# Infini-attention with a routed token: SP in emitted order, reordered projection jobs, and reads apart from writes

## The chip, the cores and the metric

The kernel runs on one core of one Trainium2 chip, in one launch. The metric is the device time of the launch in microseconds. The kernel before was timed in three runs: 855.94 us median (854.62 to 859.12). The profile that is read here is of one more execution, which took 853.65 us; its span, from the first recorded instruction to the last, is 851.4 us.

## The reference

```python
x = A_x                                   # 2048 tokens x 640, float32
g = sigmoid((x * gate_w).sum(-1, keepdims=True))
q, k, v = (heads of x @ wq, x @ wk, x @ wv)   # 32 heads of 20 columns, 4 segments of 512 tokens
for s in range(4):                        # M, z start at zero
    p = softmax(qs @ ks.T * scale + causal_mask)
    a_dot = p @ vs
    a_mem = phi(qs) @ M / (phi(qs) @ z + 1e-6)
    o_s = sig(beta) * a_mem + (1 - sig(beta)) * a_dot
    M += phi(ks).T @ vs ;  z += phi(ks).sum()
a = concat(o_s) @ wo
r = x @ w_r ; t = argmax(r)               # one routed token
y = (silu(x[t] @ w_gate) * (x[t] @ w_up)) @ w_down * sigmoid(r[t])
out = g * a + (1 - g) * (x with y added to row t)
```

## The kernel before

Products are kept near float32 by splitting each operand into `hi` (rounded) and `lo` (the rest), and adding three matrix products: hi·hi, hi·lo, lo·hi. The core runs everything on one stream of TensorE (PE) work, written out by hand.

**Units and jobs.** The heads are taken in two halves of 16, and in each half the four segments follow one another: 8 units `u`. The projections of a unit are nine jobs of 15 matmuls each, in the order `JOBS`: five jobs T0 to T4 (128 rows of q and k columns by 512 tokens, `acc` at L338) and four jobs V0 to V3 (128 tokens by 320 columns of v, `acc` at L343). `TILES` says which heads a T job holds; group 0 of the unit is complete after T1, group 1 after T2, group 2 after T3, group 3 after T4 (`LAST`).

**From a T job to the attention.** When a T job is done, `evac_t` writes `hi` (ScalarE, ACT) and `lo` (VectorE, DVE), and `place` stores both to a scratch in DRAM (`stkq`, `stkk`: L214, L216). When a group's q or k is complete there, `place` reads it back, rearranged, as the operands `qs` and `ks` (L220). There are `NS` = 5 such buffers for each.

**Groups and slots.** A group `n` is four heads of one segment, 32 in all. The main loop goes through groups in six slots each. In a slot `b_step` makes scores of group n (`bt`, L414; ACT takes their exponentials `p`, GpSimd, POOL, masks them), `a_step` makes scores of a group ahead, from which DVE takes the row maxima (`a` L383, `junk` L386), and `fill` emits projection matmuls until their progress in groups (`chunks`) is `LEAD` = 3.4 groups ahead of the slot. The maxima of group n+1 are split (`m_split`, `mneg`) in slot 3, transposed on PE (`m_rows`, `mtp` L399) in slot 4, copied by ACT (`mr`) and written by four small DMAs into two rows of that group's `qs` (L404). The first `bt` of group n+1 needs them. `pv_step` multiplies the exponentials with v in slots 5 and 1; `norm` divides in slot 2 and stores the group to DRAM (`otok`, L462).

**The rest.** At group 15 `route` finds the routed token, with eight small DMAs that each need the one before (`rrow`, `row`, `sel`, `all`, twice); from group 16 on the three products of its SwiGLU run beside the attention, with weights loaded in pairs (`wt`, L521). From group 28 on `out_proj` multiplies the stored rows with `wo`: for each 128 tokens it loads `ot` and `xf` (`row_load`, `out_load`), transposes (`ttp`, L600), multiplies (L625) and stores (L634). At the start of each of its four segments the loads and the transposes are emitted one right behind the other.

**What sets the order.** All DMAs are issued by SyncE (SP), one after the other: an issue whose data or buffer isn't ready holds all that stand behind it. PE alone runs in the order in which the program emits its instructions (`manual_schedule`, L85). For SP, DVE, ACT and POOL a scheduler sorts the instructions, by its own estimate of when each can start. At the start `prepare_t` loads and splits the weights of all five T jobs (a group's columns once for each job that needs a part of them), and those of V, before the first matmul is emitted (L664 to L672).

Of the kernel before, what the change touches and what calls it, by code (L numbers as in the profile page):

```python
# [18 lines left out]
KT = D // 128  # L19
# [24 lines left out]
)  # L44
QGROUP = {0: 0, 1: 1, 3: 2, 4: 3}
JOBS = ("T0", "T1", "V0", "V1", "T2", "V2", "V3", "T3", "T4")
LAST = {"T1": 0, "T2": 1, "T3": 2, "T4": 3}


# [5 lines left out]
def tile_infini_mod(  # L55
# [26 lines left out]
    def f32(t):  # L82
        return t.bitcast(F32)

    ctx.enter_context(tc.manual_schedule(engines={mybir.EngineType.PE}))  # L85


    jp = one.tile([128, 128], I32, name="jp")
# [73 lines left out]

    def prepare_t(hf, j, eng=None):

        hi, lo = w_tile(("T", hf, j))
        for i, (r0, r1, kind, g, c0) in enumerate(TILES[j]):
            t = pool.tile([128, KT, 4, DH], F32, tag="raw", bufs=4, name="raw")
            nc.sync.dma_start(t.rearrange("p k j d -> p k (j d)"), columns(kind, hf, g, GC).rearrange("(k p) m -> p k m", p=128))
            src = t[:, :, :, c0 // 4:(c0 + r1 - r0) // 4].rearrange("p k j d -> p k d j")
            h_, l_ = (f32(w).rearrange("p (k m) -> p k m", k=KT)[:, :, r0:r1].rearrange("p k (d j) -> p k d j", j=4)  # L170
                      for w in (hi, lo))
            split(h_.bitcast(F32R), l_.bitcast(F32R), src, eng or nc.vector)

    def load_w(key):
        if key[0] == "V":
# [31 lines left out]

    def place(kind, m, c0, hi, lo, r0, n):

        assert m - NS < current[0]  # L210
        d = stk[kind][m % NS]
        first, gap, low = {"q": (0, GC, 2 * GC), "k": (0, 2 * GC, GC)}[kind]
        src = f32(hi)[r0:r0 + n, :L]
        nc.sync.dma_start(bass.AP(tensor=d.tensor, offset=d.offset + (first + c0) * L, ap=[[L, n], [gap * L, 2], [1, L]]),  # L214
                          bass.AP(tensor=src.tensor, offset=src.offset, ap=[list(src.ap[0]), [0, 2], list(src.ap[1])]))
        nc.sync.dma_start(d[low + c0:low + c0 + n, :], f32(lo)[r0:r0 + n, :L])  # L216
        if c0 + n == GC:
            dst = f32((qs if kind == "q" else ks)[m % NS])
            for b in range(2):
                nc.sync.dma_start(dst[64 * b:64 * b + ST].rearrange("r p t -> r (p t)"),  # L220
                                  d.rearrange("(r b p) t -> r b (p t)", b=2, p=2)[:, b])
# [77 lines left out]
    def prefetch(u, job):  # L299

        hf, s = divmod(u, SEG)
        if s == SEG - 1:
            at = {"T0": 0, "T1": 1, "T2": 2, "T3": 3, "T4": 4}.get(job)
            if at is not None and hf + 1 < NH:
                prepare_t(hf + 1, at)
            elif at is not None:
                load_w(("O", at))
                split_w(("O", at))
        if u + 1 < NU:
            for k in {"T3": (0, 1), "T4": (2, 3, 4)}.get(job, ()):  # L310
                load_x(u + 1, k)
                if k < 2:
                    split_x(u + 1, k)
        if u == SEG and job == "T0":
            for k in range(KT):
                load_w(("V", 1, k))
                split_w(("V", 1, k))

    def projections():
        total = 15 * (5 * L + 4 * VC)  # L320
        old = 0
        for u in range(NU):
            hf, s = divmod(u, SEG)
            done = 0
            for job in JOBS:
                j = int(job[1])
                prefetch(u, job)
                acc = psum.tile([128, L], F32, tag="misc", bufs=3, name="acc")
                w = L if job[0] == "T" else VC + (2 if hf == 0 else 0)
                more = rest(old)  # L330
                i = 0
                for k in range(KT):
                    xh, xl = X[u, k]
                    for part in range(3):
                        if job[0] == "T":
                            wh, wl = (t[:, 128 * k:128 * k + 128] for t in W["T", hf, j])
                            a, b = ((wh, xh), (wl, xh), (wh, xl))[part]
                            nc.tensor.matmul(acc, a, b, start=i == 0, stop=i == 3 * KT - 1)  # L338
                        else:
                            wh, wl = (t[:, :w] for t in W["V", hf, k])  # L340
                            h_, l_ = xh[:, 128 * j:128 * j + 128], xl[:, 128 * j:128 * j + 128]
                            a, b = ((h_, wh), (h_, wl), (l_, wh))[part]
                            nc.tensor.matmul(acc[:, :w], a, b, start=i == 0, stop=i == 3 * KT - 1)  # L343
                        i += 1
                        done += w
                        chunks[0] = 4 * (u + min(done / total, 1.0))
                        yield w * COST_MM
                        if i in (4, 7, 10, 13):
                            cost = next(more, 0.0)
                            if cost:  # L350
                                yield cost
                    if job == "T4" and u + 1 < NU and k < 3:
                        split_x(u + 1, k + 2)
                yield from more
                old = len(tail)
                if job[0] == "T":
                    evac_t(u, j, acc)
                else:
                    evac_v(u, j, acc)
                if job in LAST:  # L360
                    groups[0] = 4 * u + LAST[job] + 1
                if job == "T4" and s < SEG - 1:
                    tail.append(memory_write(u))
        yield from rest(len(tail))
        chunks[0] = 4.0 * NU + 100
# [81 lines left out]
    def norm(n):  # L447
# [10 lines left out]
        nc.vector.tensor_tensor(out=ou, in0=tp[:, :, :, :DH], in1=sub(rs, 0, [[4, 4], [1, 4], [0, DH]]), op=OP.mult)  # L458
        if s > 0:
            nc.gpsimd.tensor_tensor(out=ou, in0=ou, in1=om.pop(n), op=OP.add)  # L460
        c0 = DH * (HH * hf + 4 * g)
        nc.sync.dma_start(otok[L * s:L * s + L, c0:c0 + GC].rearrange("(c p) e -> p c e", p=128),  # L462
                          ou.rearrange("p c j d -> p c (j d)"))

# [200 lines left out]
    for k in range(KT):  # L665
        load_x(0, k)
        split_x(0, k, nc.vector if k % 2 else nc.gpsimd)
    for j in range(1, KT):
        prepare_t(0, j)
        if j == 1:  # L670
            for k in range(KT):
                load_w(("V", 0, k))  # L672
                split_w(("V", 0, k))
    proj = Fill(projections())

    extra = []
    side = []
    LEAD = 3.4

    def fill(at):  # L680
        proj.until(lambda: chunks[0] >= at / 6 + LEAD)
# [16 lines left out]
    for n in range(-2, NG):  # L698
        for slot in range(6):
# [13 lines left out]
            if n >= -1:  # L713
                fill(6 * n + slot)
            if slot == 3 and 0 <= n + 1 < NG:
                m_split(n + 1)
            if slot == 4 and 0 <= n + 1 < NG:
                m_rows(n + 1)
            if n >= -1:
                fill(6 * n + slot + 0.5)  # L720
            if n >= 1 and slot == 2:
                norm(n - 1)
                ready[0] = n - 1
            if n == 15 and slot == 0:
                route()
# [8 lines left out]

    pv_step(NG - 1, 1)
    extra[0].run(4000)
    norm(NG - 1)
    ready[0] = NG - 1
    extra[0].finish()
    Fill(out_proj(3)).finish()  # L740
# [40 lines left out]
```

## Time and profile before

| | |
|---|---|
| median of 3 runs | 855.94 us |
| profiled execution: its time, its span | 853.65 us, 851.4 us |
| PE busy | 701.1 us (82%) |
| DVE, ACT, POOL busy | 453.7 (53%), 360.5 (42%), 188.9 (22%) us |
| mean granted clock of PE | 0.895 of 2.4 GHz |
| DMA moved | 117.95 MB, 139 GB/s mean |
| chain that ended last | PE 51%, DMA 23%, DVE 9%, ACT 7%, SP 5% |

How to read it: PE is busy most of the span, so time is lost where it stands still, and where its clock is granted at half. "A <- B" means that A's engine stood idle until B was done. A bracket at the end of a timeline row is that idle time. SPq is SP's issue of DMAs; a row of several issues lasts as long as they took together, waits between them included. Where an issue waits, the row before ends and the next one starts late.

### The profile page before, as it was taken

The page shows a single profiled execution, that of the slowest core. Times are in us where ns is not written, and L with a number is a line of the kernel's source. Part 1 is how long each engine was busy: PE and PEld are TensorE (multiplying, and loading weights), DVE is VectorE, ACT ScalarE, POOL GpSimd, SP SyncE. Part 2 cuts the span into 40 slices and gives each one's busy share as a digit, 9 for nine tenths or more (in the row PEclk, how much of TensorE's full clock was granted, in tenths as well). Part 3 has the DMA queues.
Part 4 walks back from the last instruction along what each step waited for, and adds up shares of the span by engine and source line. Part 5 has one row for each costly group of instructions (what it writes and reads, how often), then busy time and mean ns, then how long its engine had stood idle before and what let it go on. Part 6 is the DMA issues. An engine that isn't in the chain of part 4 may idle for free.

```text
span 851.4 us, 13366 instructions
## 1 busy us (share of the span) xinstructions
PE 701.1 (82%) x4496; PEld 469.2 (55%) x4496; DVE 453.7 (53%) x1523; ACT 360.5 (42%) x608; POOL 188.9 (22%) x297
## 2 busy tenths in 40 slices
PE   5067789987998899668978889777988998899998
PEld 2045356644754565435644555445554665777787
DVE  6324546555555566345654546563564666474354
ACT  4312434454544455344443434433452545344422
POOL 4010412142213233322231111331241222111100
PEclk9569889988998999679988989889997999799999
DMA  6632633264426445566246635665445565443453
GB/s 181 178 117 61 185 113 94 70 175 137 103 70 171 112 114 148 144 173 137 70 125 175 195 118 157 197 194 155 118 113 155 156 161 164 115 142 104 146 178 125
DMA packets 85876, 117.95 MB, mean 139 GB/s; under 512 B 42726, under 2 KB 46320, under 8 KB 85808
## 3 DMA queue, kind: packets, MB, share of 16 engines
q1 hardware_dynamic: 85808, 117.10, 49.3%
q8 instruction: 36, 0.59, 0.3%
q14 instruction: 32, 0.26, 0.1%
HBM read 74.58 MB, written 41.96 MB: 137 GB/s over the span
## 4 chain that ended last, share of the span: by engine, by line
PE 51%; DMA 23%; DVE 9%; ACT 7%; SPq 5%; issue 4%; POOL 0%; ACTq 0%; DVEq 0%
PE acc L338 13%; PE acc L343 7%; PE pv L434 6%; PE acc L625 6%; PE bt L414 6%; DMA ks<-stkk 6%; PE a L383 5%; DVE junk L386 4%; DMA qs<-mr 4%; DMA stkq<-lo 3%; DMA stkk<-lo 3%; DMA xf<-in_x_dram 2%; SPq L220 2%; PE nm L253 2%; SPq L404 2%
## 5 line engine op out<-in xcount | busy, mean ns | idle before, releaser
L386 DVE CUSTOM_DVE_ANT_0 junk<-a,mask 128x512 bf16<-128x512 f32 (+3 forms) x512 | 250.6, 489 | 178.7 <-PE a L383 168.2
L418 ACT ACTIVATE p<-bt 128x768 f32<-128x768 f32 (+1 forms) x192 | 169.6, 883 | 211.4 <-PE bt L414 209.0
L421 POOL TENSOR_SCALAR_AFFINE_SELECT p<-p 128x256 f32<-128x256 f32 (+1 forms) x192 | 94.6, 493 | 421.3 <-ACT p L418 417.8
L383 PE MATMUL a<-ks,qs 60*128 60x256 f32 (+2 forms) x512 | 98.1, 375 | 73.8 <-DMA ks<-stkk 55.0
L414 PE MATMUL bt<-qs,ks 62*128 62x256 f32 (+2 forms) x512 | 105.9, 425 | 40.8 <-DMA qs<-mr 34.1
L414 PEld LDWEIGHTS bt<-qs,ks 62*128 62x128 f32 x512 | 50.1, 199 | 101.5 <-issue 61.2
L383 PEld LDWEIGHTS a<-ks,qs 60*128 60x128 f32 x512 | 54.3, 204 | 91.5 <-issue 38.4
L338 PE MATMUL acc<-xhi,whi 128*128 128x512 f32 x200 | 92.3, 461 | 9.2 <-ACT xhi L148 8.0
L338 PE MATMUL acc<-xhi,wlo 128*128 128x512 f32 x200 | 94.7, 474 | 0.2 <-DVE wlo L149 0.2
L338 PE MATMUL acc<-xlo,whi 128*128 128x512 f32 x200 | 92.4, 462 | 1.2 <-POOL xlo L149 1.0
L434 PE MATMUL pv<-p,va 128*32 128x512 f32 (+3 forms) x1024 | 87.9, 465 | 0.0
L149 POOL TENSOR_TENSOR xlo<-raw,xhi 128x512 fp32r<-128x512 f32 x38 | 48.2, 1275 | 76.6 <-ACT xhi L148 72.2
L338 PEld LDWEIGHTS acc<-xhi,whi 128*128 128x128 f32 x200 | 42.4, 212 | 30.6 <-issue 14.5
L343 PE MATMUL acc<-wlo,xhi 128*128 128x322 f32 (+1 forms) x160 | 56.5, 353 | 0.0
L338 PEld LDWEIGHTS acc<-xlo,whi 128*128 128x128 f32 x200 | 42.4, 212 | 23.7 <-issue 15.3
L625 PE MATMUL acc<-whi,oh 128*128 128x320 f32 x160 | 53.3, 333 | 2.3 <-ACT oh L602 1.1
L343 PE MATMUL acc<-whi,xhi 128*128 128x322 f32 (+1 forms) x160 | 54.6, 341 | 0.3 <-ACT mr L401 0.3
L343 PE MATMUL acc<-whi,xlo 128*128 128x322 f32 (+1 forms) x160 | 52.0, 325 | 0.0
L625 PE MATMUL acc<-whi,ol 128*128 128x320 f32 x160 | 51.7, 323 | 0.3 <-DVE ol L603 0.3
L338 PEld LDWEIGHTS acc<-xhi,wlo 128*128 128x128 f32 x200 | 43.3, 217 | 15.6 <-issue 9.3
L434 PEld LDWEIGHTS pv<-p,va 128*32 128x32 f32 x1024 | 28.3, 115 | 40.2 <-issue 30.1
L625 PE MATMUL acc<-wlo,oh 128*128 128x320 f32 x160 | 50.2, 313 | 0.0
(104 smaller groups left out, 923.8 us busy)
## 6 DMA issues: line engine op xcount, KB each, us to landing
qs<-stkq SPq DMA_DIRECT2D x64, 240.0 KB
ks<-stkk SPq DMA_DIRECT2D x64, 240.0 KB
raw<-in_xT_dram SPq DMA_DIRECT2D x40, 256.0 KB
stkq<-hi SPq DMA_DIRECT2D x32, 320.0 KB
stkq<-lo SPq DMA_DIRECT2D x32, 160.0 KB
otok<-ou SPq DMA_DIRECT2D x32, 160.0 KB
ot<-otok SPq DMA_DIRECT2D x16, 320.0 KB
xf<-in_x_dram SPq DMA_DIRECT2D x16, 320.0 KB
```

Source lines behind the costliest of these rows:

```text
L149: eng.tensor_tensor(out=lo, in0=raw, in1=f32(hi), op=OP.subtract)
L220: nc.sync.dma_start(dst[64 * b:64 * b + ST].rearrange("r p t -> r (p t)"), d.rearrange("(r b p) t -> r b (p t)", b=2, p=2)[:, b])
L253: nc.tensor.matmul(nm[:, c, :], e[:GC, 128 * c:128 * c + 128], mbd[:, g, :], start=True, stop=True)
L338: nc.tensor.matmul(acc, a, b, start=i == 0, stop=i == 3 * KT - 1)
L343: nc.tensor.matmul(acc[:, :w], a, b, start=i == 0, stop=i == 3 * KT - 1)
L383: nc.tensor.matmul(a[:, b, at:at + nw], q_, k_, start=True, stop=True)
L386: nc.vector.tensor_tensor_reduce(out=junk[:, :w], in0=a[:, b, at:at + w], in1=mask[:, L - w:], scale=1.0, scalar=-3e38, op0=OP.add, op1=OP ...
L414: nc.tensor.matmul(bt[:, b, at:at + nw], k_, q_, start=True, stop=True)
L418: nc.scalar.activation(pt, bt[:, :, at:at + w], AF.Exp, scale=SCALE)
L421: nc.gpsimd.affine_select(out=d, in_=d, pattern=[[0, 2], [0, k], [1, 128]], base=0, channel_multiplier=-1, compare_op=OP.is_ge, fill=0.0)
L434: nc.tensor.matmul(pv[n][32 * j:32 * j + 32, L - w:], va[u % 2][:, c, VW * h:VW * h + 32], pt_tiles[n, j % 2, min(c, 2)][:, j // 2, at:at ...
L625: nc.tensor.matmul(acc[:, :n], a_[:, 128 * k:128 * k + 128], b_[:, n * b:n * b + n], start=i == 0, stop=i == 3 * KT - 1)
```

## The change

SP, too, keeps the order in which the program emits. With that the program emits its DMAs elsewhere: weights are loaded by groups of heads (`READY`; one load feeds every T job that holds a part), and those of the first unit job by job ahead of their use; `place` only writes, and the reads of the operands are gathered (`backs`) and emitted by `bring_back` at the sixth matmul of the next job, from where on the group counts as landed. `JOBS` and the prefetches are reordered, `LEAD` is 3.7, `m_split` and `m_rows` stand one slot earlier, and the store of a group one slot after its `norm`.

```diff
+READY = (("q", 0), ("k", 0)), (("q", 1), ("k", 1)), (("k", 2),), (("q", 2), ("k", 3)), (("q", 3),)
-JOBS = ("T0", "T1", "V0", "V1", "T2", "V2", "V3", "T3", "T4")
+JOBS = ("T0", "T1", "T2", "V0", "V1", "T3", "V2", "T4", "V3")
...
-    ctx.enter_context(tc.manual_schedule(engines={mybir.EngineType.PE}))
+    ctx.enter_context(tc.manual_schedule(engines={mybir.EngineType.PE, mybir.EngineType.SP}))
...
     def prepare_t(hf, j, eng=None):
-        hi, lo = w_tile(("T", hf, j))
-        for i, (r0, r1, kind, g, c0) in enumerate(TILES[j]):
+        for kind, g in READY[j]:
             t = pool.tile([128, KT, 4, DH], F32, tag="raw", bufs=4, name="raw")
...
+            for i, tl in enumerate(TILES):
+                for r0, r1, kind_, g_, c0 in tl:
+                    if (kind_, g_) != (kind, g):
+                        continue
+                    hi, lo = W.get(("T", hf, i)) or w_tile(("T", hf, i))
...
     def place(kind, m, c0, hi, lo, r0, n):
...
         if c0 + n == GC:
+            backs.append((kind, m))
+
+    backs = []
+
+    def bring_back():
+        while backs:
+            kind, m = backs.pop(0)
+            assert m - NS < current[0]
+            d = stk[kind][m % NS]
             dst = f32((qs if kind == "q" else ks)[m % NS])
             for b in range(2):
                 nc.sync.dma_start(dst[64 * b:64 * b + ST].rearrange("r p t -> r (p t)"),
                                   d.rearrange("(r b p) t -> r b (p t)", b=2, p=2)[:, b])
...
     def prefetch(u, job):
-            at = {"T0": 0, "T1": 1, "T2": 2, "T3": 3, "T4": 4}.get(job)
+            at = {"T1": 0, "T2": 1, "V0": 2, "V2": 3, "V3": 4}.get(job)
...
-            for k in {"T3": (0, 1), "T4": (2, 3, 4)}.get(job, ()):
+            for k in {"T4": (0, 1), "V3": (2, 3, 4)}.get(job, ()):
...
-        if u == SEG and job == "T0":
-            for k in range(KT):
-                load_w(("V", 1, k))
-                split_w(("V", 1, k))
+        if u == 0:
+            j = {"T0": 1, "T1": 2, "V0": 3, "V1": 4}.get(job)
+            if j is not None:
+                prepare_t(0, j)
...
+                        if i == 6:
+                            bring_back()
+                            groups[0] = landed
+                            if (u, job) in ((0, "T2"), (SEG, "T0")):
+                                for kk_ in range(KT):
+                                    load_w(("V", hf, kk_))
+                                    split_w(("V", hf, kk_))
...
-                    groups[0] = 4 * u + LAST[job] + 1
+                    landed = 4 * u + LAST[job] + 1
...
-    for j in range(1, KT):
-        prepare_t(0, j)
-        if j == 1:
-            for k in range(KT):
-                load_w(("V", 0, k))
-                split_w(("V", 0, k))
...
-    LEAD = 3.4
+    LEAD = 3.7
...
             if slot == 3 and 0 <= n + 1 < NG:
-                m_split(n + 1)
-            if slot == 4 and 0 <= n + 1 < NG:
                 m_rows(n + 1)
             if n >= -1:
                 fill(6 * n + slot + 0.5)
+            if slot == 2 and 0 <= n + 1 < NG:
+                m_split(n + 1)
             if n >= 1 and slot == 2:
-                norm(n - 1)
+                done = norm(n - 1)
+            if n >= 1 and slot == 3:
+                store(n - 1, done)
                 ready[0] = n - 1
```

Three places on SP show what moves. The first is the start of the program: the rows up to the first store of an operand, of the kernel before and then of the changed one (`raw<-in_wc` is a load of weights, `stkq`, `stkk` the scratch, `qs`, `ks` the operands).

```order
L168 DMA raw_242<-in_wc_dram 128x5x80
L168 DMA raw_246<-in_wc_dram 128x5x80
L168 DMA raw_252<-in_wc_dram 128x5x80
L168 DMA raw_256<-in_wc_dram 128x5x80
L214 DMA stkq0_71<-hi_276 80x2x512
L216 DMA stkq0_71<-lo_277 80x512
L214 DMA stkk0_76<-hi_276 48x2x512
L216 DMA stkk0_76<-lo_277 48x512
L220 DMA qs0_106<-stkq0_71 60x1024 x2
```

```order
L168 DMA raw_176<-in_wc_dram 128x5x80
L168 DMA raw_180<-in_wc_dram 128x5x80
L218 DMA stkq0_71<-hi_204 80x2x512
L220 DMA stkq0_71<-lo_205 80x512
L218 DMA stkk0_76<-hi_204 48x2x512
L220 DMA stkk0_76<-lo_205 48x512
L168 DMA raw_216<-in_wc_dram 128x5x80
L233 DMA qs0_106<-stkq0_71 60x1024 x2
L218 DMA stkq1_72<-hi_242 80x2x512
```

Before, 25 issues of weights stand between the last load of `xT` and the first store; now two do. The second place is in unit 1, where a T job's operands are stored and read, with the four small writes of the maxima (`qs<-mr`) behind them; of the kernel before, then of the changed one.

```order
L214 DMA stkq2_73<-hi_1472 80x2x512
L216 DMA stkq2_73<-lo_1473 80x512
L214 DMA stkk2_78<-hi_1472 48x2x512
L216 DMA stkk2_78<-lo_1473 48x512
L220 DMA qs2_112<-stkq2_73 60x1024 x2
L220 DMA ks2_113<-stkk2_78 60x1024 x2
L404 DMA qs0_106<-mr_1493 1x8x128 x4
```

```order
L218 DMA stkq2_73<-hi_1373 80x2x512
L220 DMA stkq2_73<-lo_1374 80x512
L218 DMA stkk2_78<-hi_1373 48x2x512
L220 DMA stkk2_78<-lo_1374 48x512
L144 DMA raw_1385<-in_xT_dram 128x512
L144 DMA raw_1387<-in_xT_dram 128x512
L144 DMA raw_1389<-in_xT_dram 128x512
L233 DMA qs2_112<-stkq2_73 60x1024 x2
L233 DMA ks2_113<-stkk2_78 60x1024 x2
L424 DMA qs0_106<-mr_1500 1x8x128 x4
```

The reads stood right behind the writes that they need, and the maxima right behind the reads; now three loads stand between writes and reads. The third place is the last segment of `out_proj`: loads of the rows (`ot`, `xf`) of its first 128 tokens (7754 and 7756 before, 7738 and 7740 now) against the stores of the results of the segment before it (7601 and 7667 before, 7575 and 7651 now).

```order
L445 DMA ot_7754<-otok_66 128x640
L588 DMA xf_7756<-in_x_dram 128x640
L634 DMA out_0_dram<-xf_7601 128x640
L445 DMA ot_7773<-otok_66 128x640
L588 DMA xf_7775<-in_x_dram 128x640
L634 DMA out_0_dram<-xf_7667 128x640
```

```order
L658 DMA out_0_dram<-xf_7575 128x640
L658 DMA out_0_dram<-xf_7651 128x640
L465 DMA ot_7738<-otok_66 128x640
L612 DMA xf_7740<-in_x_dram 128x640
L465 DMA ot_7757<-otok_66 128x640
L612 DMA xf_7759<-in_x_dram 128x640
```

Before, the loads went ahead of the last two stores; now they follow both.

## Rows read from the trace of the kernel before

**Rows 1.** Waits of PE: us in total, times, longest us.
```profile
PE a L383 <- DMA ks<-stkk: 55.0, 16, 23.4
PE bt L414 <- DMA qs<-mr: 34.1, 13, 7.8
PE a L383 <- DVE mx L386: 17.4, 13, 5.7
PE bt L414 <- ACT p L418: 6.4, 7, 1.3
```
**Rows 2.** Timeline of the start: start us, us, engine, line, instruction.
```profile
15.73 0.59 ACT L227 CAST hi<-acc 128x512 fp32r<-128x512 f32 x1 [1.04 <-PE acc L338]
22.26 9.27 SPq L168 DMA_DIRECT2D raw<-in_wc_dram  x7
23.35 0.69 DVE L228 TENSOR_TENSOR lo<-acc,hi 128x512 fp32r<-128x512 f32 x1 [2.72 <-ACT hi L227]
...
41.92 0.78 SPq L220 DMA_DIRECT2D ks<-stkk  x2
46.27 1.71 PE L383 MATMUL a<-ks,qs 60*128 60x512 f32 x2 [23.43 <-DMA ks<-stkk]
```
**Rows 3.** Timeline of unit 2, around its third group's operands and maxima.
```profile
258.14 0.53 SPq L216 DMA_DIRECT2D stkk<-lo  x1
260.05 0.77 SPq L220 DMA_DIRECT2D qs<-stkq  x2
265.37 0.76 PE L383 MATMUL a<-ks,qs 60*128 60x512 f32 x1 [4.04 <-DMA ks<-stkk]
271.11 0.22 PE L399 MATMUL mtp<-identr,mneg 128*66 128x128 f32 x1
275.74 2.70 SPq L404 DMA_DIRECT2D qs<-mr  x4
280.07 0.85 PE L414 MATMUL bt<-qs,ks 62*128 62x512 f32 x2 [3.04 <-DMA qs<-mr]
```
**Rows 4.** Timeline of a group whose maxima weren't late.
```profile
231.81 0.22 PE L399 MATMUL mtp<-identr,mneg 128*66 128x128 f32 x1
236.15 0.62 PE L414 MATMUL bt<-qs,ks 62*128 62x512 f32 x2
```
**Rows 5.** Timeline around the routing, on SP.
```profile
335.66 0.38 SPq L469 DMA_DIRECT2D rrow<-best  x1
343.34 0.25 SPq L471 DMA_DIRECT2D row<-rrow  x1
372.43 0.43 SPq L477 DMA_DIRECT2D sel<-top  x1
374.36 0.35 SPq L479 DMA_DIRECT2D all<-sel  x1
```
**Rows 6.** Busy time by stretch: PE, PEld, DVE, ACT, POOL, granted clock, DMA share, GB/s.
```profile
265.30:270.50 5.20, 4.95 (x14) 2.79 (x14) 1.74 (x5) 0.75 (x2) 0.00 (x0) 0.50 0.51 126
```
**Rows 7.** Timeline of the tail: loads, last product of a segment, next transposes, store.
```profile
814.80 0.33 SPq L588 DMA_DIRECT2D xf<-in_x_dram  x1
818.05 0.83 ACT L589 ACTIVATE xf<-xf,gb 128x640 f32<-128x640 f32 x1 [2.89 <-DMA xf<-in_x_dram]
819.93 0.32 SPq L445 DMA_DIRECT2D ot<-otok  x1
825.52 0.71 PE L600 MATMUL ttp<-identf,ot 128*128 128x128 f32 x5
826.69 0.38 SPq L634 DMA_DIRECT2D out_dram<-xf  x1
```
**Rows 8.** Split of the maxima on DVE: durations min/median/max in ns.
```profile
L394 DVE TENSOR_SCALAR mneg<-mx x32: 109/168/1241, 70.9 to 775.0; 128x16 fp32r<-128x16 f32 x32
```
**Rows 9.** Timeline: GpSimd beside the longest of these.
```profile
261.29 2.49 POOL L149 TENSOR_TENSOR xlo<-raw,xhi 128x512 fp32r<-128x512 f32 x2
261.34 1.24 DVE L394 TENSOR_SCALAR mneg<-mx 128x16 fp32r<-128x16 f32 x1
```

More of the change, by code (lines that the diff above doesn't have):

```diff
@@ L163, in prepare_t @@
     def prepare_t(hf, j, eng=None):
-        hi, lo = w_tile(("T", hf, j))
-        for i, (r0, r1, kind, g, c0) in enumerate(TILES[j]):
+        for kind, g in READY[j]:
             t = pool.tile([128, KT, 4, DH], F32, tag="raw", bufs=4, name="raw")
             nc.sync.dma_start(t.rearrange("p k j d -> p k (j d)"), columns(kind, hf, g, GC).rearrange("(k p) m -> p k m", p=128))
[L169 to L172, printed above, removed]
+            for i, tl in enumerate(TILES):
[3 more added lines that the diff above has]
+                    hi, lo = W.get(("T", hf, i)) or w_tile(("T", hf, i))
+                    src = t[:, :, :, c0 // 4:(c0 + r1 - r0) // 4].rearrange("p k j d -> p k d j")
+                    h_, l_ = (f32(w).rearrange("p (k m) -> p k m", k=KT)[:, :, r0:r1].rearrange("p k (d j) -> p k d j", j=4)
+                              for w in (hi, lo))
+                    split(h_.bitcast(F32R), l_.bitcast(F32R), src, eng or nc.vector)
     def load_w(key):
@@ L208, in place @@
     def place(kind, m, c0, hi, lo, r0, n):
-        assert m - NS < current[0]
         d = stk[kind][m % NS]
@@ L313, in prefetch @@
                     split_x(u + 1, k)
-        if u == SEG and job == "T0":
-            for k in range(KT):
-                load_w(("V", 1, k))
-                split_w(("V", 1, k))
+        if u == 0:
+            j = {"T0": 1, "T1": 2, "V0": 3, "V1": 4}.get(job)
+            if j is not None:
+                prepare_t(0, j)
     def projections():
         total = 15 * (5 * L + 4 * VC)
-        old = 0
+        old = landed = 0
         for u in range(NU):
@@ L351, in projections @@
                                 yield cost
-                    if job == "T4" and u + 1 < NU and k < 3:
+                    if job == "V3" and u + 1 < NU and k < 3:
                         split_x(u + 1, k + 2)
@@ L360, in projections @@
                 if job in LAST:
-                    groups[0] = 4 * u + LAST[job] + 1
-                if job == "T4" and s < SEG - 1:
+                    landed = 4 * u + LAST[job] + 1
+                if job == "V3" and s < SEG - 1:
                     tail.append(memory_write(u))
@@ L460, in norm, with store @@
             nc.gpsimd.tensor_tensor(out=ou, in0=ou, in1=om.pop(n), op=OP.add)
-        c0 = DH * (HH * hf + 4 * g)
+        return ou
+    def store(n, ou):
+        hf, s = divmod(n // 4, SEG)
+        c0 = DH * (HH * hf + 4 * (n % 4))
         nc.sync.dma_start(otok[L * s:L * s + L, c0:c0 + GC].rearrange("(c p) e -> p c e", p=128),
@@ L736, in tile_infini_mod @@
     extra[0].run(4000)
-    norm(NG - 1)
+    store(NG - 1, norm(NG - 1))
     ready[0] = NG - 1
```

## The prediction

> **What bounds the kernel now.** I read the table of time first: PE is busy 82% of 851.4 us, so some 150 us are its own waits, and its clock is 0.895 of full. Next the waits of PE, which say for whom it stands [rows 1]: 55.0 us for reads of the operands (`ks<-stkk`), 34.1 us for the maxima (`qs<-mr`), 17.4 us for DVE and 6.4 us for ACT. Then the timelines of the longest. The one wait of 23.4 us lies in the start. There `hi` of the first job is ready at 15.73 + 0.59 = 16.3 us, but SP issues loads of weights until 22.26 + 9.27 = 31.5, and only then the first store; the first `a` starts at 46.27 [rows 2]. The other waits come in pairs, one pair in nearly every unit, at the third group, whose T job is emitted last before its use. SP issues the last write at 258.14 + 0.53 = 258.7, waits 1.4 us for it to land, then reads, and `a` stands until 265.37. The same happens once more 12 us later: the maxima are transposed at 271.11, but SP, which waits for writes and issues reads, comes to them at 275.74 only, and `bt` stands until 280.07 [rows 3]. So SP's order, and how short before their use the DMAs are emitted, bound this kernel at these places; elsewhere PE's work does.
>
> **The change part by part.** The terms are in us of the profiled execution, 853.65; the median shown is 2.3 above it.
>
> *The start: -12.* Two loads are left ahead of the first stores. The second job's `lo` is ready at 23.35 + 0.69 = 24.0 [rows 2]. Its stores are then issued one after the other, four more at 0.53 (the row of 258.14): 26.2. Then 1.4 to land, 0.77 for the read of q [rows 3], which gives 28.4 for the issue of `ks`; from there to `a` it took 46.27 - 41.92 = 4.35 [rows 2]: 32.7. The stores and reads of the first job and the next load of weights are now among them, for which I add 1.5: 34, so 12 less. Bounds: -6, if the weights that now come job by job hold PE, to -15. The larger lead lets PE work through some more jobs before the first `bt`; these come off later, so they cost nothing.
>
> *The operands: -30.* The other waits for `ks` are 55.0 - 23.4 = 31.6 [rows 1]. By the emitted order a group counts as landed after the sixth matmul of the next job, and `LEAD` and the order of jobs put the third group's T job sixth instead of eighth of nine, and 0.3 groups earlier beside. The wait was 4.04 in a unit [rows 3]; the room gained is more than one V job and 0.3 groups, of the order of 10 us. I take 1.6 us as left. Bounds -24 to -31.6.
>
> *The maxima: -22.* Without the routing's (7.8, below) there are 34.1 - 7.8 = 26.3 [rows 1]. Where nothing disturbs, they take 236.15 - 231.81 = 4.34 from transposition to `bt`, with no wait at all [rows 4], so there is no slack. In the disturbed group it took 280.07 - 271.11 = 8.96, since SP was 275.74 - 271.11 = 4.6 late [rows 3]. The transposition moves by one slot; 4.34 us are about 1.6 slots, so a slot is 2.7 and the new room is 7.0. The reads before the maxima no longer wait for fresh writes, as six matmuls and their slots lie between. I leave 4 us as residue. Bounds 0 to -26.
>
> *The routing: +5.* Its eight DMAs now stand in one piece on SP, with nothing between. From the rows: `rrow` holds what follows 343.34 - 335.66 = 7.7, `sel` 374.36 - 372.43 = 1.9 [rows 5]; for `row` I take an estimate of 2.9 and for `all` that of `sel`. Twice 7.7 + 2.9 + 1.9 + 1.9 is 29 us in which SP issues nothing else, starting about 0.35 of a group before group 15. Behind it stand six writes, four reads and two loads (some 8 us) and then the maxima of group 16. These land after 29 + 8 + 4.3 = 41, where PE would want them after about 1.35 groups, 22 to 24: PE loses 17 to 19, waits for DVE on the way included. Before, the routing cost 5.7 + 7.8 = 13.5 [rows 1], so +5. Bounds -8 to +15.
>
> The Trainium skill ("DMA: Bandwidth & Descriptors", section "Anatomy of one DMA") gives a fixed cost of about 2.0 us for a DMA, nearly independent of what it does. By that the eight would take 16 us and this term would be -6, not +5. The trace differs: `rrow` took 7.7 us [rows 5], and I go by it.
>
> *The clock: -20.* After the wait that ends at 265.37 PE has a granted clock of 0.50 for 5.2 us [rows 6], so 2.6 us of work are lost there. Of 29 waits for operands and maxima [rows 1] about 14 are long and go; where the clock fell within the wait less is lost, so I take 1.4 each. Bounds -10 to -30.
>
> *Gaps between jobs: -6.* Where PE had run ahead to finish a T job, `fill` had nothing left for a slot, and PE waited for ACT and DVE: 6.4 + 17.4 - 5.7 = 18 [rows 1], some 5 of it in the start. With the longer lead the program is not forced ahead. Bounds 0 to -13.
>
> *The tail: +24.* This is what the change loses. At the start of each of the four segments of `out_proj` the transposes follow the last product at once, and the row that they need is loaded by DMA. Before, the scheduler had put that load 825.52 - 819.93 = 5.6 us ahead [rows 7]. Now it stands behind the store of the rows just done, which is issued at 826.69, 1.2 us after the last product. Add 0.4 to issue and 818.05 - 814.80 = 3.25 for such a load: 826.69 + 0.4 + 3.25 = 830.3 against 825.52, some 4.5 us of PE for each of four segments, 18. Within a segment the load has 21 products of room, which hides it beside the attention and misses by 1 in the last few rows: 3. Half clock afterwards: 3. Bounds 0, if SP runs far enough ahead, to +38.
>
> *The split of the maxima: +4.* `m_split` and `m_rows` move together, so `mtp` follows the last `junk` after some 3.4 us instead of 5.8 (by one slot of 2.7). The two splits take 0.17 us each as a rule [rows 8], which fits. The longest took 1.24, while GpSimd split `xlo` beside it for 2.49 [rows 9]: there PE would wait 1 to 2 us. The median of 0.168 says that this hits a few groups only. Bounds 0 to +20.
>
> The Trainium skill has the reason ("SBUF — State Buffer", section "Who interferes with whom"): VectorE and GpSimd share a pair of ports as an exclusive lock, and the loser waits for the winner's whole instruction. The trace agrees, 1.24 us against 0.168; the rule speaks against the change, since it moves a PE instruction close behind a DVE instruction that can be locked out.
>
> *Rest: +4* (0 to +15): loads of x and of the SwiGLU's weights, which SP can no longer issue early, and weights of the start.
>
> Sum: -12 - 30 - 22 + 5 - 20 - 6 + 24 + 4 + 4 = -53. 853.65 - 53 = 800.7; with the 2.3 between that execution and the median 803.
>
> **Rivals.**
> *SP becomes the bound (slower).* In emitted order everything on SP waits for the slowest in front. Some 20 of the 32 groups have reads right before their maxima. If SP is late there by more than the new room, PE stands in 20 groups instead of 8. With a wait as in rows 3, 3.04, and 1.4 of clock, these cost 20 x 4.4 = 89, while the gain of 22 and half of the clock's 20 are not had: 803 + 89 + 32 = 924 at worst; at 1.3 us of wait it is 803 + 54 + 10 = 867, which is where it decides. For it: the maxima had no slack. Against: a slot of 2.7 is added for each. I give 0.07, at about 875.
> *The splits hold PE.* If DVE is late for `mtp` in every group, not a few, with 1.2 us each: 32 x 1.2 - 4 = 34 more, 837, or 845 with some half clock. For it: the longest split; against: the median [rows 8]. 0.13.
> *The tail doesn't lose.* If SP runs ahead of PE far enough to load early, and the clock stays up: 803 - 24 - 10 = 769. For it: the loads need only a free buffer; against: the stores in front wait for DVE. 0.25.
> *The change doesn't reach the waits.* If the operands land as late as before, because DMAs are slower once more of them run together, only start, routing and tail remain: 856 - 12 + 5 + 24 = 873, or with half of the gains 838. 0.10, half of it near 856.
> *The forecast:* 0.45, with 785 to 822 as its own range.
>
> **How the numbers follow.** A median within 0.5%, 851.7 to 860.2, can't be told from no change. Slower: the first rival's 0.07 and a little of the fourth, 0.09. Same: 0.04. Faster: 0.87. The range reaches down to the third rival, 763, and up to the second and half of the fourth, 845.
>
> **What would show it.** Right: the first `a` before 36 us; no wait of `a` for `ks` above 1 us after the start; at most a few waits of `bt` for `mr`, one long one of 7 to 18 at group 16; a clock above 0.92; waits of `ttp` for `ot` at the segment starts, 4 to 5 us each; a few of `mtp` for `mneg`. Wrong: waits for `mr` in most groups, PE waiting for `xhi` or weights in each unit, or a tail without waits.

## The result, and the profile after

The changed kernel took 823.76 us (median of 4 runs, 812.46 to 825.51), the kernel before 856.53 beside it. The ratio is 0.957, 95% interval 0.947 to 0.967. The forecast was 803 us, range 763 to 845: the direction was right, the gain some 20 us smaller. The profiled execution took 825.51 us, with a span of 823.8. It is the slowest of the four, and the ratios, unlike the medians, leave disturbed runs out, so the spans read below show a gain of 27.6 us where the ratio gives some 37.

First the waits of PE, in the changed kernel (total us, times, longest):

```profile
PE ttp L624 <- DMA ot<-otok: 29.6, 8, 10.1
PE bt L434 <- DMA qs<-mr: 23.3, 4, 19.1
PE a L403 <- DVE mx L406: 16.0, 19, 4.1
PE acc L351 <- ACT xhi L149: 15.1, 8, 7.2
PE acc L351 <- ACT whi L149: 9.1, 3, 4.9
PE a L403 <- DMA ks<-stkk: 3.3, 2, 2.9
PE bt L434 <- ACT p L438: 2.1, 3, 1.0
```

Against [rows 1], the operands have gone from 55.0 to 3.3 us. The maxima fell from 34.1 to 23.3, and 19.1 of these are one wait. New at the top is `ttp` for `ot`, 29.6. Next the timeline of SP and PE in a calm group after, which answers to [rows 3] and [rows 4]:

```profile
152.91 0.53 SPq L220 DMA_DIRECT2D stkk<-lo  x1
153.54 1.75 SPq L144 DMA_DIRECT2D raw<-in_xT_dram  x3
155.46 0.79 SPq L233 DMA_DIRECT2D qs<-stkq  x2
...
157.90 0.22 PE L419 MATMUL mtp<-identr,mneg 128*66 128x128 f32 x1
158.44 2.80 SPq L424 DMA_DIRECT2D qs<-mr  x4
...
160.71 0.51 PE L434 MATMUL bt<-qs,ks 62*128 62x256 f32 x4
```

Loads of x stand between the last write and the first read, SP is free when the maxima come (158.44, right behind 157.90), and no `bt` waits. Now the two places that lost. The timeline of SP and PE around the routing, which answers to [rows 5]:

```profile
358.12 0.48 SPq L493 DMA_DIRECT2D rrow<-best  x1
...
376.82 0.34 SPq L493 DMA_DIRECT2D rrow<-best  x1
383.98 0.24 SPq L495 DMA_DIRECT2D row<-rrow  x1
...
388.80 0.34 SPq L503 DMA_DIRECT2D all<-sel  x1
...
395.59 2.68 SPq L424 DMA_DIRECT2D qs<-mr  x4
401.26 1.17 PE L434 MATMUL bt<-qs,ks 62*128 62x512 f32 x2 [19.14 <-DMA qs<-mr]
```

And the start of the last segment of `out_proj`, which answers to [rows 7]:

```profile
788.34 0.34 SPq L658 DMA_DIRECT2D out_dram<-xf  x1
788.77 0.38 SPq L465 DMA_DIRECT2D ot<-otok  x1
791.93 1.30 PE L624 MATMUL ttp<-identf,ot 128*128 128x128 f32 x5 [4.21 <-DMA ot<-otok]
```

The load of `ot` is issued 0.43 us behind the store, and 3.2 us before its use, not 5.6 us as before. Last, two stretches (us of PE, PEld, DVE, ACT and POOL with instructions, granted clock, DMA share, GB/s). Of the kernel before:

```profile
100.00:360.00 260.00, 225.42 (x1465) 145.26 (x1464) 146.87 (x539) 123.73 (x210) 68.35 (x107) 0.91 0.46 123
706.00:851.40 145.40, 131.30 (x899) 105.34 (x897) 74.76 (x204) 54.40 (x91) 18.53 (x33) 0.96 0.45 139
```

and of the changed kernel:

```profile
100.00:360.00 260.00, 238.78 (x1608) 154.69 (x1608) 160.08 (x611) 140.68 (x237) 77.20 (x120) 0.94 0.52 138
635.50:823.80 188.30, 145.82 (x907) 116.44 (x905) 76.22 (x207) 54.26 (x91) 19.59 (x35) 0.85 0.33 106
```

The last line of each starts with the `mtp` of group 28. The middle does 1608 matmuls where it did 1465 (10% more). The tail takes 188.3 us where it took 145.4, and its clock is 0.85 where it was 0.96.

The starts of `mtp` tell how far the changed kernel is ahead at each group (us; `mtp` itself stands one slot, 2.7 us, earlier in its group after):

| group | 0 | 5 | 9 | 15 | 17 | 28 | end of span |
|---|---|---|---|---|---|---|---|
| before | 77.2 | 185.8 | 271.1 | 407.7 | 448.6 | 706.0 | 851.4 |
| after | 66.0 | 157.9 | 232.9 | 353.9 | 412.1 | 635.5 | 823.8 |
| ahead | 11.2 | 27.9 | 38.2 | 53.8 | 36.5 | 70.5 | 27.6 |

So the gain grows steadily, the routing (groups 15 to 17) takes 17 back, and the tail takes 43 back, of which 40 are left after the shift of `mtp`.

### The profile page after: what moved, and what is told of

The parts are those of the page before. It is cut to its first block, busy times and chain, and to the rows that moved or that the text cites. A ratio compares the mean times of both kernels' runs of the same rounds, so it can differ in the third digit from the quotient of the medians.

```text
span 823.8 us, 13347 instructions
## 1 busy us (share of the span) xinstructions
PE 691.1 (84%) x4496; PEld 468.9 (57%) x4496; DVE 442.0 (54%) x1523; ACT 361.6 (44%) x608; POOL 188.7 (23%) x297
## 4 chain that ended last, share of the span: by engine, by line
PE 52%; DMA 19%; DVE 9%; ACT 7%; issue 6%; SPq 4%; POOL 1%; POOLq 0%; DVEq 0%; ACTq 0%
PE acc L351 13%; PE pv L454 7%; PE acc L649 7%; PE bt L434 7%; PE acc L356 7%; PE a L403 5%; DVE junk L406 3%; DMA xf<-in_x_dram 3%; DMA raw<-in_xT_dram 3%; DMA qs<-mr 3%; DMA stkq<-lo 3%; PE nm L266 3%; DVE lo L241 2%; DMA rrow<-best 2%; ACT hi L240 1%
## 5 line engine op out<-in xcount | busy, mean ns | idle before, releaser
L434 PE MATMUL bt<-qs,ks 62*128 62x256 f32 (+2 forms) x512 | 100.0, 421 | 25.4 <-DMA qs<-mr 23.3
L351 PE MATMUL acc<-xhi,whi 128*128 128x512 f32 x200 | 89.7, 449 | 24.2 <-ACT xhi L149 15.1
L403 PE MATMUL a<-ks,qs 60*128 60x256 f32 (+2 forms) x512 | 84.7, 361 | 20.8 <-DVE mx L406 16.0
L434 PEld LDWEIGHTS bt<-qs,ks 62*128 62x128 f32 x512 | 47.1, 198 | 82.5 <-issue 41.5
L454 PE MATMUL pv<-p,va 128*32 128x512 f32 (+3 forms) x1024 | 85.3, 452 | 0.0
L403 PEld LDWEIGHTS a<-ks,qs 60*128 60x128 f32 x512 | 50.3, 202 | 33.2 <-DVE mx L406 22.5
L351 PEld LDWEIGHTS acc<-xhi,whi 128*128 128x128 f32 x200 | 41.1, 206 | 45.9 <-ACT xhi L149 17.4
L649 PE MATMUL acc<-whi,oh 128*128 128x320 f32 x160 | 57.9, 362 | 4.9 <-ACT oh L626 3.4
L649 PE MATMUL acc<-whi,ol 128*128 128x320 f32 x160 | 56.1, 351 | 0.4 <-DVE ol L627 0.2
L351 PEld LDWEIGHTS acc<-xlo,whi 128*128 128x128 f32 x200 | 41.1, 205 | 25.2 <-issue 15.1
L649 PE MATMUL acc<-wlo,oh 128*128 128x320 f32 x160 | 54.7, 342 | 0.0
L351 PEld LDWEIGHTS acc<-xhi,wlo 128*128 128x128 f32 x200 | 41.5, 207 | 15.9 <-issue 10.1
```

The source lines that it names most:

```text
L403: nc.tensor.matmul(a[:, b, at:at + nw], q_, k_, start=True, stop=True)
L434: nc.tensor.matmul(bt[:, b, at:at + nw], k_, q_, start=True, stop=True)
L454: nc.tensor.matmul(pv[n][32 * j:32 * j + 32, L - w:], va[u % 2][:, c, VW * h:VW * h + 32], pt_tiles[n, j % 2, min(c, 2)][:, j // 2, at:at ...
L649: nc.tensor.matmul(acc[:, :n], a_[:, 128 * k:128 * k + 128], b_[:, n * b:n * b + n], start=i == 0, stop=i == 3 * KT - 1)
```

## The experiments

Differences are taken between ratios to the kernel before and turned into us with 854, about its time in all sets; the changed kernel is 817 by that, good to some 9 us.

**e1: the tail's loads earlier.**

```diff
...
-            if t < 4 * s + 3:
-                row_load(t + 1)
-                out_load(t + 1)
+            load_rows(t + 1)      # also of the next segment, if its rows are stored
...
                         rows = out_rows(t + 1)
+                        load_rows(t + 2)
```

> The changed kernel, in which out_proj loads the rows of otok and x of the next row tile a tile earlier than it does: right after the transposes of the present one, ahead of the store of the rows just done, and across the border of a segment where those rows are ready. Theory A (the tail gives back some 40 us because each segment's first load stands behind the store): the eight waits of ttp for ot, 29.6 us, fall below 6, the clock of the last 184 us rises from 0.85 to over 0.92, and the time falls from 824 to 784-800. Rival B (the tail is slow for the clock or the transfers, whatever their order): waits for ot move into waits for xf or for the store, and the time stays at 815-825. Rival C (the loads ahead now hold the attention's own stores and maxima): waits of bt for mr appear behind 650 us, time 805-830.

Measured: 782.6 us (ratio 0.915, 0.911 to 0.919), 36 us less. Of the waits for `ot` one is left, the very first one, of 10.0 us (below 6 in all was expected). That wait, and the last stretch, from group 28 on, of this kernel:

```profile
PE ttp L624 <- DMA ot<-otok: 10.0, 1, 10.0
```

```profile
628.40:778.90 150.50, 130.26 (x907) 105.17 (x905) 76.03 (x207) 54.50 (x91) 19.66 (x35) 0.94 0.42 133
```

The waits are 19.6 less. The same 907 matmuls take 130.3 us instead of 145.8, at a clock of 0.94 instead of 0.85. A holds, but for the first wait.

**e2: the routing spread.**

```diff
-            if n == 15 and slot == 0:
-                route()
+            if (n, slot) == (13, 0):
+                routing = Fill(route())   # yields 4 slots behind rrow, 2 behind row, sel and all
+            if 13 <= n < 16:
+                routing.run(1.0)
...
```

> The changed kernel, in which the routing's eight DMAs are emitted one by one over three groups (from group 13 on, four slots after a write of 128 values, two after any other), not in one piece at group 15. Theory A (SP issues nothing while each of the eight waits for the one before): the waits of a for mx (4.07) and bt for mr (19.14) at group 16 go, no wait above 2 us between groups 13 and 17, and the time falls by 10-18, from 824 to 806-814. Rival B (a write of 128 single values of 4 bytes holds the DMA queues themselves, wherever it stands): waits of 4-8 us appear at two groups of 13 to 15 instead, and the time stays at 818-826.

Measured: 797.4 us (0.932, 0.928 to 0.936), 22 less. The first write and its read, and the waits for the maxima, in this kernel:

```profile
333.71 0.38 SPq L493 DMA_DIRECT2D rrow<-best  x1
...
337.90 6.52 SPq L424 DMA_DIRECT2D qs<-mr  x4
...
346.80 0.35 SPq L497 DMA_DIRECT2D row<-rrow  x1
```

```profile
PE bt L434 <- DMA qs<-mr: 8.5, 6, 2.9
```

Fifteen other DMAs stand between `rrow` and `row` now, where SP had stood waiting. The waits for `mr` are 8.5 us in all, 2.9 the longest. A holds in kind: the two waits are gone, one of 2.9 us at group 16 stands in their place, and the time is below A's range.

**e3: both.** The two edits together.

> The changed kernel with both edits, the loads of out_proj a tile earlier and the routing's DMAs spread. Theory A (two losses that do not touch each other): 824 less 25-40 less 10-18, that is 768-788. Rival B (the routing's time is taken back, since PE that comes to the tail earlier finds the SwiGLU's rows or the stores late): no better than the early tail alone, 784-800.

Measured: 761.4 us (0.891, 0.887 to 0.894), 57 less; the parts give 36 + 22 = 58. The gains add up, so A holds: two separate losses. The time is below its range, since the routing gives more than it expected.

**e4: the old start.**

```diff
+    for j in range(1, KT):
+        prepare_t(0, j)       # all weights of the first half ahead of the first job
...
```

> The changed kernel with the old start: all weights of Q, K and V of the first half are emitted before the first job, as before the change. Theory A (the start is worth what the first product shows, 46.3 against 29.9 us, of which 3-4 us are worked off again as lead): first a at 44-50 us, time 834-842. Rival B (PE uses the wait in the start to run ahead with jobs that it has to do anyway, so a late first a costs little): 822-830. Rival C (in emitted order the weights hold up more than before, since the scheduler no longer puts stores among them): first a later than 52, time above 842.

Measured: 815.3 us (0.953, 0.948 to 0.958), not to be told from the changed kernel. The timeline of its start:

```profile
39.03 0.76 PE L399 MATMUL a<-ks,qs 60*128 60x512 f32 x1 [10.36 <-DMA ks<-stkk]
66.07 0.23 PE L415 MATMUL mtp<-identr,mneg 128*66 128x128 f32 x1
```

and of the changed kernel's, with the stretch between the two instructions behind it:

```profile
29.92 0.72 PE L403 MATMUL a<-ks,qs 60*128 60x512 f32 x1 [2.88 <-DMA ks<-stkk]
53.74 0.65 PE L351 MATMUL acc<-xhi,whi 128*128 128x512 f32 x1 [4.90 <-ACT whi L149]
66.05 0.31 PE L419 MATMUL mtp<-identr,mneg 128*66 128x128 f32 x1
```

```profile
29.90:66.05 36.15, 24.31 (x96) 17.62 (x97) 16.35 (x53) 10.86 (x22) 0.00 (x0) 0.74 0.46 109
```

The first `a` is 9.1 us later, yet the first `mtp` starts at the same time. Of the 9.1 us the changed kernel gives back 4.9 in the wait for weights shown, and 3.6 in slower matmuls: the same 96 take 24.31 us at a mean clock of 0.74, with the old start 20.73 at 0.79. B holds in kind, a little below its range. That `a` would start at 39 no theory expected, so the 7 us from 46 to 39 have another cause in the change, which stays open.

**e5: the scheduler's order for SP again.**

```diff
-    ctx.enter_context(tc.manual_schedule(engines={mybir.EngineType.PE, mybir.EngineType.SP}))
+    ctx.enter_context(tc.manual_schedule(engines={mybir.EngineType.PE}))
```

> The changed kernel, but SP's instructions are again put in order by the scheduler, as before the change; all else as changed. Theory A (jobs, lead and the split of reads from writes make the steady gain; SP's emitted order is what costs in the routing and the tail): group 28's maxima stay near 635 us, the waits of ttp for ot fall below 8, time 770-795. Rival B (SP's emitted order makes the steady gain, since the scheduler puts writes ahead of reads and maxima that PE stands for): waits of bt for mr of 15 us and more come back, group 28 later than 665, time 825-850.

Measured: 748.7 us (0.878, 0.872 to 0.883), 68 less than the changed kernel: the emitted order costs 68 us, and the rest of the change gains 105. No wait of `ttp` for `ot` is left. The waits for the maxima, of which the longest is in the routing, and the last stretch from group 28 on:

```profile
PE bt L434 <- DMA qs<-mr: 11.5, 3, 10.2
610.40:748.20 137.80, 127.61 (x906) 102.98 (x906) 72.90 (x204) 52.29 (x88) 18.73 (x33) 0.98 0.43 132
```

So 50.5 of the traces' 75.6 us lie in the tail, the rest before it. A holds for what the emitted order costs in the tail, and B falls. But A expected group 28 near 635, and it comes at 610.4: the emitted order holds the steady part and the routing back too, by 25 us, of which 3.5 were there at group 0.

**e6: before, with SP in emitted order.** The same line, changed in the kernel before.

> The kernel before, with SP in emitted order and nothing else of the change. Theory A (the order alone brings nothing in the steady part, and loses 25-40 in the tail and some in the start, where all weights now stand ahead of the first store): first a later than 50 us, waits of ttp for ot near 30, time 870-900. Rival B (SP's emitted order makes the steady gain): the waits of a for ks and bt for mr after the start fall from 66 us in all to below 30, time 820-850.

Measured: 963.0 us (1.132, 1.124 to 1.140), 13% slower than before. The waits:

```profile
PE a L383 <- DMA ks<-stkk: 76.6, 16, 26.5
PE bt L414 <- DMA qs<-mr: 60.0, 15, 18.7
```

A's direction, at a higher price: operands and maxima get worse, 136.6 us against 89.1 in [rows 1], and PE waits 31.8 for `ot`.

**e7: reads at once, in emitted order.**

```diff
             backs.append((kind, m))
+            bring_back()          # and groups[0] is set with the job, not six matmuls later
...
```

> The changed kernel, but the reads of operands are emitted right behind their writes, and a group counts as landed with its job, as before the change. Theory A (reads behind fresh writes hold SP some 1.4 us each, and the maxima stand behind them): the waits of bt for mr beside the routing's rise from some 4 us to 12-25, those of a for ks to 5-15, group 28 later by 15-30, time 832-850. Rival B (the order of the jobs and the lead alone give the room): group 28 within 6 us of 635, time 812-824.

Measured: 918.3 us (1.076, 1.069 to 1.084), 102 more than the changed kernel and slower than before. A piece of the timeline of SP and PE in this kernel:

```profile
178.07 0.77 SPq L234 DMA_DIRECT2D ks<-stkk  x2
178.88 1.33 SPq L144 DMA_DIRECT2D raw<-in_xT_dram  x3
183.54 0.79 PE L352 MATMUL acc<-xhi,whi 128*128 128x512 f32 x1 [5.37 <-ACT xhi L149]
```

the waits of SP for the second part of a write, ahead of its read:

```profile
SPq L234 <- DMA stkq<-lo: 83.3, 32, 5.4
SPq L234 <- DMA stkk<-lo: 72.5, 30, 4.1
```

and the waits of PE:

```profile
PE bt L433 <- DMA qs<-mr: 55.4, 16, 20.9
PE acc L352 <- ACT xhi L149: 49.9, 8, 7.9
PE a L402 <- DMA ks<-stkk: 7.0, 1, 7.0
```

So SP stands 62 times, for 2.5 us in the mean, between a write and its read; with the waits for `hi` it is 180.6 us for operands' writes, where it is 27.5 in the changed kernel. Behind such pairs come the loads of x (178.88, right behind a read) and the maxima, and these are late (`xhi` 49.9 against 15.1), not the operands: their one wait is that of the first `a`. A holds in kind; the place was half foreseen, the size was not.

**e8: the maxima one slot later, in emitted order.**

```diff
-            if slot == 3 and 0 <= n + 1 < NG:
+            if slot == 4 and 0 <= n + 1 < NG:
                 m_rows(n + 1)
-            if slot == 2 and 0 <= n + 1 < NG:
+            if slot == 3 and 0 <= n + 1 < NG:      # stands ahead of the second fill, as before
                 m_split(n + 1)
```

> The changed kernel, but the split of the maxima and their transposition stand one slot later, as before the change. Theory A (the slot of 2.7 us is the room that the maxima lacked): waits of bt for mr rise from some 4 us beside the routing's to 15-30, group 28 later by 10-25, time 828-845. Rival B (SP, which no longer waits for writes there, was all that made the maxima late): no wait for mr above 2.5 us beside the routing's, time 812-824.

Measured: 831.4 us (0.976, 0.968 to 0.985), 16 more, a little beyond the uncertainty of some 11. The waits that A names are there, 29.0 us beside the longest, and the `mtp` of group 28 comes 12.4 us later (647.9), of which 2.7 are the slot by which it now stands later:

```profile
PE bt L434 <- DMA qs<-mr: 47.4, 14, 18.4
```

**e9: reads at once, in the scheduler's order.** The edit of the reads on top of the scheduler's order.

> The changed kernel with SP's order again the scheduler's and the reads of operands right behind their writes, both as before the change. Theory A (reads apart from writes matter only in emitted order, where a read that waits holds everything behind it; the scheduler moves other DMAs in between by itself): within 1.5% of 749, that is 740-760. Rival B (they give the operands room in any order): waits of a for ks and bt for mr after the start rise from 11.5 to 25-50, time 770-810.

Measured: 760.6 us (0.891, 0.884 to 0.897), 11 more than with the reads apart. That is at A's edge, just beyond it: worth 102 us in emitted order, the reads apart are worth some 11 in the scheduler's.

**e10: old jobs, in the scheduler's order.** The prefetches move with the jobs. In this kernel no job follows the last T job, so the four reads of the last group's operands are left out.

```diff
-JOBS = ("T0", "T1", "T2", "V0", "V1", "T3", "V2", "T4", "V3")
+JOBS = ("T0", "T1", "V0", "V1", "T2", "V2", "V3", "T3", "T4")
...
```

> The changed kernel with SP's order again the scheduler's and the jobs of a unit in their old order (T0 T1 V0 V1 T2 V2 V3 T3 T4), at the new lead of 3.7. Theory A (the third group's operands were late for the order of the jobs): waits of a for ks of 2-4 us return in most units, 15-30 in all, time 775-805. Rival B (the lead of 3.7 covers it, whatever the order): no such waits after the start, time 742-758.

Measured: 765.5 us (0.898, 0.891 to 0.905), 17 more, between the two theories. Eight waits for operands return, 9.6 us beside the start's 10.0:

```profile
PE a L403 <- DMA ks<-stkk: 19.6, 9, 10.0
```

**e11: the maxima one slot later, in the scheduler's order.**

> The changed kernel with SP's order again the scheduler's, and the maxima's split and transposition one slot later, as before the change. Theory A (the maxima had no slack, and the slot is their room in any order): waits of bt for mr rise from 11.5 to 25-50, time 765-790. Rival B (under the scheduler's order the maxima pass ahead of other DMAs, and the slot is worth little): 745-758.

Measured: 734.7 us (0.854, 0.846 to 0.861), 21 less than with them early, and the fastest kernel here. Both theories fall: neither expected a gain. Its milestones show where: 10.1 us between groups 15 and 17 (41.5 against 51.6) and 5.5 after group 28, of which 2.7 are the slot by which `mtp` stands later here. The wait for `mr` of 10.2 us that stood in the routing is gone; the longest is now 2.8:

```profile
PE bt L434 <- DMA qs<-mr: 11.5, 10, 2.8
```

The scheduler has placed the routing's DMAs otherwise: it issues the first `rrow` at 310.79, 32 us before the `mtp` of group 15, where without this edit it comes behind it. That the slot itself is worth anything here isn't shown: up to group 15 the two kernels are even, once the slot is taken off.

**e12: all three.** The scheduler's order, with the tail's loads early and the routing spread.

> The changed kernel with SP's order again the scheduler's, the loads of out_proj a tile earlier and the routing's DMAs spread over three groups. Theory A (what the scheduler leaves is the routing's wait of 11.2 us near 380 us and its clock; the tail's loads are early by themselves): 733-742. Rival B (the scheduler has put the routing's DMAs where they do least, and the spread only brings them among others): 745-755.

Measured: 743.8 us (0.870, 0.864 to 0.876), 7 less, within the uncertainty, and between the two theories. The wait in the routing goes (3.3 us for `mr` in all), the tail had nothing left to give.

## Why the prediction was right, and where it was short

**Operands (-30): right.** The 3.3 us that are left are the start's own two waits. Of the reasons the order of the jobs is shown in part: with the reads at once no such wait returns (e7: the start's alone), with the old order of jobs eight do (e10), but at 9.6 us, not the 31.6 of before. What the longer lead gives was not tried apart.

**Maxima (-22): right in size.** Beside the routing's 19.1 they fell from 26.3 to 4.2, the residue that was put at 4. Two causes were named, the slot and the reads that no longer stand before the maxima. In emitted order both are needed: with the slot taken away these waits are 29.0 us (e8), with the reads at once 34.5 (e7: 55.4 less 20.9, its wait in the routing). In the scheduler's order the slot does not lessen them (11.5 us in e5 and in e11).

**Routing (+5): the mechanism right, the size wrong.** The eight DMAs took 31.0 us (358.12 to 389.14) where 29 was forecast. The loss was worked out as 17 to 19 us of PE; the waits measured 19.14, and 4.07 for `mx`. Charged with 13.5 of the old waits that makes +9.7. The clock was left out: in 360 to 420 us it was 0.86 before and 0.77 after, and by the milestones the routing took 17 back. So +17. (At the 2.0 us for each DMA that the prediction sets against its own price, the same sum gives -8, not -6.)

**Tail (+24): the mechanism right, the size wrong.** Three of the four segment starts wait 4.09, 4.34 and 4.21 us against 4.5 forecast. The first waits 10.1, so 22.8 in place of 18, and 6.8 inside segments in place of 3. That first wait is another one than was forecast: no store stands in front, but SP issues the load only behind a T job's writes and reads, while PE stands from 647.0 on, and e1 leaves the wait as it is.

```profile
649.78 0.76 SPq L233 DMA_DIRECT2D ks<-stkk  x2
650.59 0.39 SPq L465 DMA_DIRECT2D ot<-otok  x1
657.11 1.33 PE L624 MATMUL ttp<-identf,ot 128*128 128x128 f32 x5 [10.12 <-DMA ot<-otok]
```

The term "Half clock afterwards: 3" is the one that failed most: the matmuls (907 where it was 899) were busy 14.5 us longer than before (145.8 against 131.3) at 0.85 of the clock. In all +40. Some of this belongs to the execution that was profiled: in e4, whose tail is the same, the stretch takes 183.6 us, the matmuls 11.3 us longer than before at 0.87, which makes +36.

**Start (-12): wrong in what it was worth.** The first `a` came at 29.9 (forecast 34), but e4 shows that this is worked off by the first `mtp`. The wait for weights 24 us later took part of its place, which was costed as "if the weights that now come job by job hold PE". At group 0 the changed kernel is ahead by 11.2, 8.5 without the shift of `mtp`, and just as far with the old start: another part of the change gives that.

**Clock (-20): in part.** It rose in the middle (0.91 to 0.94 in 100 to 360) and fell in routing and tail: 0.901 over the span, not above 0.92.

**Gaps (-6): right.** 6.4 + 17.4 before, 2.1 + 16.0 after: 5.7. **Split of the maxima (+4):** `mtp` did wait, 8.0 us in five places, but for DVE's other work (`ou`, `phi`, `ol`), never for `mneg`, whose longest splits took 0.486 and 0.449 us. A split of 1.24 us was not met again.

**Rest (+4): the size right, made up otherwise.** Of the kernel before:

```profile
PE acc L338 <- ACT xhi L148: 8.0, 2, 7.4
PE acc L338 <- ACT whi L148: 1.3, 1, 1.3
```

After, they are 15.1 and 9.1 us, 14.9 more in all; PE's waits for the SwiGLU's weights fell from 9.7 to 0.4. The prediction has "PE waiting for `xhi` or weights in each unit" among its signs of being wrong. It is there in small: eight waits for `xhi`, 7.2 us of them in the start.

**The sum.** Routing and tail were short by 12 and 16. With these in place of the forecast's terms, -53 becomes -25, and the spans differ by 27.6. The terms of the steady part come to -82 in the forecast; measured are 67.8 at group 28 (70.5 less the slot) and the 17 of the routing: 85. That these agree is in part luck: the start's term was worth nothing by its own cause, the causes of the operands' term are shown in part only, and the emitted order, which the forecast charged with nothing here, held the groups back (e5).

**The rivals.** *SP becomes the bound* has the right mechanism: without the reads apart it happens (e7: 918, e6: 963), at more than the 875 that it was given. (Its price at the point where it decides, 867, leaves out the 22 of the maxima that its own condition takes away.) *The splits hold PE* did not come about. *The tail doesn't lose* came about only in the scheduler's order (e5). *The change doesn't reach the waits* did not come about: of those for operands 3.3 us are left. The forecast treated the emitted order as a cost in routing, tail and rest alone; it also held back the steady part, and cost 68 us in all (e5). The Trainium skill ("DMA: Bandwidth & Descriptors", section "Anatomy of one DMA") puts about 2.0 us of fixed cost on a DMA, for DMAs that GpSimd issues; here SyncE issues them. The 2.5 us that SP waits between a write and its read in e7 are near it, the 7.3 us that it waits for `rrow` in the changed kernel are not.

What stays open: of the 105 us that the rest of the change gains in the scheduler's order, taking away reads apart or the jobs' order costs 11 and 17 each, and early maxima gain nothing. What the lead of 3.7, the weights loaded by groups or the later store are worth alone was not tried, nor how far the parts stand in for each other.

## What to carry to other kernels

An order that is written out for a DMA queue makes every wait in it a wait of all that stands behind: a read behind its own write, a chain of small round trips, a load behind a store. Before pinning a queue's order, count those pairs; here there were 64 pairs of write and read, at some 2.5 us each where nothing was put between them (e7), one chain of eight and the loads of fourteen tiles behind stores, and the scheduler's order beat the written one by 68 us. And a wait of PE is to be charged with the clock that it costs afterwards: in the tail 29.6 us of waits came with another 14.5 of slower matmuls, and when e1 took 19.6 of the waits away, 15.6 of busy time went with them.

## What was not expected of the hardware

A write of 128 single values (`rrow`, 0.5 KB) is slow to land, and not only its reader waited for it. The waits of SP for it, of the changed kernel and of e2:

```profile
SPq L495 <- DMA rrow<-best: 14.6, 2, 7.8
SPq L424 <- DMA rrow<-best: 3.6, 1, 3.6
```

The first is its reader, 7.3 us in the mean of two. The second is one of the four writes of the maxima (`qs<-mr`), which use nothing of it, and it is the better part of why those took 6.52 us to issue at 337.90; in the changed kernel such a row takes 2.7 us as a rule, and 4.40 at most. In e3 and e12, which spread the routing too, one such write waits 3.2 and 4.1 us for `rrow`. What ties the two together (the queue, or how the program's waits are set) was not tried.
